# Full 128-row products at unit ends, issued as two 64-row halves with a lent PSUM bank

## The chip, the cores and the metric

The kernel runs on one core of a Trainium2 chip. The metric is device time in microseconds of one execution, the median of several runs. The engines are named as the profile names them: PE (TensorE; PEld are its weight loads), DVE (VectorE), ACT (ScalarE), POOL (GpSimd), SP (SyncE, which issues most DMAs). They run side by side, each in its own program order, and wait for each other through semaphores.

## The reference

Two attention layers over the same x (2048 tokens, width 512, 32 heads of 16) are mixed token by token with a gate. A is full softmax attention. B works in four segments of 512 tokens: causal softmax attention inside a segment, plus a read of a memory that the segments before it have built.

```python
def _A_ref(x, wqkv, wo):
    ...
    scores = jnp.einsum("bhqd,bhkd->bhqk", q, k) * scale
    p = _softmax(scores, axis=-1)
    o = jnp.einsum("bhqk,bhkd->bhqd", p, v)
    return (lambda x, *d: x.transpose(*d))(o, 0, 2, 1, 3).reshape(B, S, D) @ wo

def _B_ref(x, wq, wk, wv, wo, beta):
    ...
    for s in range(N):
        qs, ks, vs = q[:, :, s], k[:, :, s], v[:, :, s]
        logits = jnp.einsum("bhqd,bhkd->bhqk", qs, ks) * scale + mask
        p = _softmax(logits, axis=-1)
        a_dot = jnp.einsum("bhqk,bhkd->bhqd", p, vs)
        ...
        o = g * a_mem + (1.0 - g) * a_dot
    ...
    return o @ wo

x = A_x
g = _sigmoid((x * gate_w).sum(-1, keepdims=True))
return g * _A_ref(x, A_wqkv, A_wo) + (1 - g) * _B_ref(x, B_wq, B_wk, B_wv, B_wo, B_beta)
```

## The kernel before, in words

**Precision.** Every product that needs full fp32 is written as three products of halves: each operand is split into a rounded fp32r part and the rest, and (rest, part), (part, rest), (part, part) are summed in one PSUM bank.

**Stages.** Up to about 280 us the kernel projects x to queries, keys and values (lines 332 to 908) and stores them in DRAM. The long part after that is the attention.

**Units, slots, bursts.** A unit is four heads of one layer for one chunk of 512 queries. A unit of A has 64 slots and a unit of B has 10; they alternate (`units`, `slots`, lines 105 to 113), so a pair has 74 slots and there are 2368 in all. The loop at line 1328 walks the slots. In slot n:

- `score_part` (line 1030) issues on PE one score product `st` (128 keys by 512 queries, 50 rows of one half of the array: rows 0 to 63 or 64 to 127), and on ACT its exponential into `p` (L1068). The scores have three PSUM banks, in the pool `st_ps`.
- `max_part` (line 263) issues on PE one product `sm` for a unit that comes LEAD = 96 slots later, in the other half of the rows, and on DVE its maxima (L275 for A; for B two masked pieces, L290, the second of them behind the next maximum of A). These have four banks, `banks`; `oldest` (line 253) picks the one whose last read was issued longest ago, by `read_last`, and `was_read` (line 257) notes a read. The maxima of a unit are needed before its scores, since they go into the rows that the exponent subtracts.
- Every third slot (BURST = 3) closes a burst. Then PE either issues values (`some_values`, line 1080: the product of `p` with v for all four heads in four column blocks, summed in the one bank `ops`), or, if the list `shared` holds anything, three products from it.

So PE runs three score-and-maximum pairs, then values or three products, and again.

**Unit ends.** When the last value of a unit is issued, `ops` is copied to `oraw` (L1106) and stored. A unit of A then fills `shared` with twelve products of 128 rows by 512 columns, which take the place of values in four bursts; this is called a group below:

- for chunk 0, `later_tile` (line 958): one tile of the queries of chunks 2 and 3. At its end (`done`) ACT copies `ops` to `full` (L962), POOL splits it, and SP stores it 12 slots later;
- for the other chunks, `output` (line 1241): half of the output product of 128 tokens of the chunk before. After the first half `keep` copies `ops` to `part` (L1259), after the second `leave` copies it to `res` (L1263), POOL adds the part (L1265), and SP stores the result 6 slots later.

All matmuls of these kinds go through the helper at line 155. The last chunk's output products use `banks` and not `ops`, at the end, when no maxima are left (`fill`, `close`).

**Order.** The order on each engine is that of the code: this is a hand-written schedule (`manual_schedule`). Work beside the loop is put into slots with `at`. `octet` (line 1138) scales eight heads of a finished pair of units on POOL and sends them through DRAM; its reciprocal is L1169. `loads` (line 319) posts the keys and queries for maxima 20 slots ahead, on SP.

Of the kernel before, what the change touches and what calls it, by code (L numbers as in the profile page):

```python
# [10 lines left out]
F32 = mybir.dt.float32  # L11
# [8 lines left out]
D = 512  # L20
# [27 lines left out]
def gated_mix(ctx, tc, x, xT, wqkv, a_wo, b_wq, b_wk, b_wv, b_wo, beta, gate_w, out):  # L48
    nc = tc.nc
# [63 lines left out]
    nS = len(slots)  # L113
# [4 lines left out]
    for k in range(NU):  # L118
# [3 lines left out]
        start, apart = (33, (3, 3)) if k == 1 else (6, (9, 3)) if k < NU - 1 else (23, (3, 3))  # L122
# [3 lines left out]
        for m in range(len(maxs), len(maxs) + 64 + 10 * len(bs)):  # L126
            r = (m + 1) % 2
# [12 lines left out]
    def raw(t):  # L140

        return t[:].bitcast(F32)
# [10 lines left out]
    def matmul(*args, **kw):  # L153

        behind[0] = nc.tensor.matmul(*args, **kw)  # L155
# [95 lines left out]
    read_last = dict(zip(range(4), range(4)))  # L251

    def oldest():

        return min(read_last, key=read_last.get)

    def was_read(b):

        if b is not None:
            read_last[b] = count[0] = count[0] + 1  # L260
# [659 lines left out]
    fr = ctx.enter_context(tc.tile_pool(name="fr", bufs=1, reuse_waits="tile"))  # L920
# [4 lines left out]
    banks = [sm_ps.tile([128, CH], F32, name=f"sm{i}") for i in range(4)]  # L925

    ops = o_ps.tile([128, CH], F32, name="ops")

    halved = {}
# [25 lines left out]
    def x_later(c):  # L955
        return xT[:, c * CH:(c + 1) * CH]

    def later_tile(c, o):

        def done():  # L960
            full = fr.tile([128, CH], F32, tag="part", name="full")
            nc.scalar.copy(full, ops)  # L962
            t = fr.tile([128, 2, 2, 2, 128], F32R, tag="blk", name="qhalves", bufs=2)
            t = t.rearrange("p a o h t -> p a (o h t)")
            nc.gpsimd.tensor_copy(t[:, 0], full)
            nc.gpsimd.tensor_sub(t[:, 1], full, t[:, 0].bitcast(F32))
            for i in range(2):
                at(n + 12, lambda i=i: nc.sync.dma_start(
                    qd["A", o, c][16 * i:16 * i + 16].rearrange("d h t -> (d h) t"), raw(t[:, i])))


            if o == NO - 1 and c == LATER[0]:
                for i in range(2):
                    load_halves(("x", LATER[1]), "B", x_later(LATER[1]), (2 * i, 2 * i + 1), n + 2 + 18 * i,
                                [n + 24 + 29 * i, n + 28 + 29 * i])
            elif o == NO - 1:
                for i, (side, w) in enumerate((("A", a_wo), ("B", b_wo))):
                    load_halves(side, side, w, (0, 1), n + 2 + 18 * i, [n + 22 + 8 * i, n + 26 + 8 * i])
                    for k in range(2, 4):
                        load_halves(side, side, w, (k,), n + 50 + 22 * i + 3 * (k - 2), [n + 62 + 18 * i + 5 * (k - 2)])  # L980

        def f(i):
            k, (a, b) = i // 3, ((1, 0), (0, 1), (0, 0))[i % 3]
            assert {("q", k), (("x", c), k)} <= ready
            matmul(ops, halved["q"][:, k, a, o * 128:(o + 1) * 128], halved["x", c][:, k, b],
                             start=(i == 0), stop=(i == 11))
            if i == 11:
                done()
        for i in range(12):
            yield lambda i=i: f(i)  # L990
# [33 lines left out]
    def from_bank(n):  # L1024

        return nc.vector.tensor_copy if n > wide.start + 4 else nc.scalar.copy
# [108 lines left out]
    def at(n, f):  # L1135
        beside.setdefault(n, []).append(f)
# [78 lines left out]
    def products(ps, t, b, side, o, start, stop):  # L1215

        assert (side, o) in ready
        for i, (x, w) in enumerate(((1, 0), (0, 1), (0, 0))):
            yield lambda i=i, x=x, w=w: matmul(ps, t[:, b, x], halved[side][:, o, w], start=start and i == 0,
                                                         stop=stop and i == 2)  # L1220

    def out_rows(c, b):
        return out[c * CH + b * 128:c * CH + (b + 1) * 128, :]
# [31 lines left out]
    part = {}  # L1255

    def keep(ps, c, b):
        part[b] = fr.tile([128, D], F32, tag="part", name="part")
        nc.scalar.copy(part[b], ps)  # L1259

    def leave(ps, c, b):
        t = fr.tile([128, D], F32, tag="res", name="res", bufs=2)
        from_bank(n)(t, ps)  # L1263
        if b in part:
            nc.gpsimd.tensor_add(t, t, part.pop(b))  # L1265
        at(n + 6, lambda: nc.sync.dma_start(out_rows(c, b), t))

# [31 lines left out]
    def close(n, side, o, b):  # L1301
        for i in range(3):
            def f(i=i):
                assert (side, o, last) in scaled
                list(products(banks[b], closed[side, o], b, side, o, (side, o) == closing[0], (side, o) == closing[-1]))[i]()
            fill.append((n, f))
# [20 lines left out]
    n = 0  # L1327
    while n < nS or queue or beside or filled[0] < len(fill):
# [5 lines left out]
        if m < nS:  # L1334
            loads(m + PRE)

            b = oldest()
# [29 lines left out]
    for b in range(4):  # L1367
# [3 lines left out]
        t = fr.tile([128, D], F32, tag="v" if b % 2 else "res", name="res", bufs=2)  # L1371
# [37 lines left out]
```

## Time and profile before

| | |
|---|---|
| median of 3 runs | 1747.57 us (1745.27 to 1747.68) |
| span of the profiled execution | 1744.5 us; what lies around it, against the median: 3.1 us |
| granted TensorE clock | 1.000 |
| exponentials, L1068 | 2261, 600 ns each |
| maxima of A, L275 | 2048, 683 ns each |
| maxima of B, L290 | 512 pieces, 482 ns each in the mean |
| products of the groups (360) | 387 to 506 ns each as recorded |
| copies of `ops` at group ends (L962, L1259, L1263) | 8 of 589 ns, 11 of 589 ns, 11 of 604 ns |

The times of one instruction go from its start to its end; the next on the same engine can start before that end, so the distance of two starts is read from the order of time. The end of a matmul is modelled. A matmul that waits for another engine shows this on its weight load (PEld). Values are recorded as two passes each.

### The profile page before, as it was taken

To read this page: it belongs to the slowest core of one execution; us is meant where nothing else is said; L and a number is where in the kernel's file an instruction comes from. 1 tells how busy PE (TensorE), PEld (TensorE's weight loads), DVE (VectorE), ACT (ScalarE), POOL (GpSimd) and SP (SyncE) were. 2 spreads that over 40 slices of the span, in tenths; PEclk is the share of its full clock that TensorE was granted. 3 is DMA by queue.
4 is the path that set the end of the run, shared out by engine and by line. 5 is a ranking of instruction groups with operands and counts; after the bars stand their busy time and mean duration, and the time that the engine had idled before them with its cause. 6 is when DMAs were issued, how large, how long until landed. Compare 5 with 4: busy or idle time off the path is not lost.

```text
span 1744.5 us, 41555 instructions
## 1 busy us (share of the span) xinstructions
PE 1738.4 (100%) x15205; PEld 885.8 (51%) x15205; DVE 1597.1 (92%) x3327; ACT 1436.5 (82%) x2763; POOL 736.5 (42%) x992
## 2 busy tenths in 40 slices
PE   9999999999999999999999999999999999999999
PEld 7887775444444444444444444444444444444445
DVE  7757788999999999999999999999999999999931
ACT  6545557888888898888888888888888888888884
POOL 3543233234352427352534353535344353535443
PEclk9999999999999999999999999999999999999999
DMA  6787567335453446454545454444445444545542
GB/s 209 251 291 227 194 226 215 110 102 145 127 153 105 138 119 183 131 137 136 143 122 157 122 143 130 134 145 122 149 130 148 130 127 124 148 115 147 149 154 63
DMA packets 149387, 261.62 MB, mean 150 GB/s; under 512 B 39064, under 2 KB 61624, under 8 KB 148672
## 3 DMA queue, kind: packets, MB, share of 16 engines
q1 hardware_dynamic: 146640, 254.42, 49.2%
q0 software_dynamic: 2400, 4.29, 0.9%
q8 instruction: 121, 1.98, 0.5%
q14 instruction: 82, 0.67, 0.1%
q10 hardware_dynamic: 144, 0.26, 0.1%
HBM read 174.39 MB, written 83.25 MB: 148 GB/s over the span
## 4 chain that ended last, share of the span: by engine, by line
PE 99%; ACT 0%; DMA 0%; DVE 0%; issue 0%; SPq 0%; ACTq 0%; DVEq 0%
PE ops L155 40%; PE st L1045 28%; PE sm L242 14%; PE pr L366 9%; PE pair L366 4%; PE sm L155 2%; PE mt_ps L232 0%; PE tps L831 0%; PE sm L1045 0%; DMA vs<-wqkv 0%; PE mps L845 0%; PE num L804 0%; PE den L808 0%; ACT p L1068 0%; DVE pm L275 0%
## 5 line engine op out<-in xcount | busy, mean ns | idle before, releaser
L1068 ACT ACTIVATE p<-st 128x512 f32<-128x512 f32 x2261 | 1190.7, 600 | 147.6 <-PE sm L242 98.6
L275 DVE TENSOR_REDUCE pm<-sm 128x1 f32<-128x512 f32 x2048 | 1276.5, 683 | 9.7 <-PE sm L242 8.7
L242 PE MATMUL sm<-kA,qA 48*128 48x512 f32 x2048 | 662.5, 424 | 0.1
L1045 PE MATMUL st<-qA,kA 50*128 50x512 f32 x2014 | 656.2, 432 | 0.0
L155 PE MATMUL ops<-p,vA 128*17 128x256 f32 (+3 forms) x6360 | 553.0, 445 | 0.0
L1045 PEld LDWEIGHTS st<-qA,kA 50*128 50x128 f32 x2014 | 326.8, 185 | 423.4 <-ACT p L1068 378.9
L242 PEld LDWEIGHTS sm<-kA,qA 48*128 48x128 f32 x2048 | 337.8, 185 | 11.3 <-DVE ph L449 3.9
L1169 POOL TENSOR_TENSOR rcp<-rec,minus 128x32 f32<-128x32 f32 x43 | 234.8, 5461 | 78.3 <-DMA rec<-dend 73.5
L290 DVE CUSTOM_DVE_ANT_0 rest<-sm,mask 128x128 f32<-128x128 f32 (+3 forms) x512 | 246.8, 482 | 0.8 <-PE sm L242 0.7
L155 PEld LDWEIGHTS ops<-p,vA 128*17 128x17 f32 x6360 | 129.2, 96 | 216.1 <-issue 185.0
L1049 POOL TENSOR_SCALAR_AFFINE_SELECT p<-p 128x512 f32<-128x512 f32 x128 | 79.4, 637 | 270.4 <-ACT p L1068 265.7
L242 PE MATMUL sm<-kB,qB 48*128 48x128 f32 (+3 forms) x512 | 166.1, 384 | 0.0
L1045 PE MATMUL st<-qB,kB 50*128 50x512 f32 (+1 forms) x495 | 105.4, 330 | 0.3 <-ACT mt L235 0.3
L1045 PEld LDWEIGHTS st<-qB,kB 50*128 50x128 f32 x495 | 68.6, 186 | 62.2 <-ACT p L1068 50.5
L155 PE MATMUL ops<-p,vB 128*17 128x128 f32 (+3 forms) x1504 | 88.3, 350 | 0.0
L242 PEld LDWEIGHTS sm<-kB,qB 48*128 48x128 f32 x512 | 79.9, 184 | 0.0
L214 POOL TENSOR_TENSOR dm<-pm 128x32 f32<-128x32 f32 x32 | 7.9, 247 | 169.9 <-DVE pm L275 169.9
L437 POOL TENSOR_SCALAR mn<-full 128x512 f32<-128x512 f32 x24 | 36.7, 1527 | 75.6 <-ACT full L432 75.6
L223 POOL CAST ms<-pm 128x16 fp32r<-128x16 f32 x32 | 6.3, 196 | 127.5 <-DVE pm L290 127.5
L1185 POOL TENSOR_TENSOR v<-v,inv 128x512 f32<-128x512 f32 x31 | 39.8, 1283 | 28.1 <-DMA inv<-rdA 21.9
L155 PEld LDWEIGHTS ops<-p,vB 128*17 128x17 f32 x1504 | 33.8, 96 | 30.1 <-issue 26.1
L440 DVE TENSOR_TENSOR q<-full,q 128x512 fp32r<-128x512 f32 x40 | 29.2, 731 | 18.6 <-ACT q L433 15.8
(319 smaller groups left out, 1690.9 us busy)
## 6 DMA issues: line engine op xcount, KB each, us to landing
kA<-kdA SPq DMA_DIRECT2D x256, 128.0 KB
vA<-vdA SPq DMA_DIRECT2D x31, 544.0 KB
kA<-kdA SPq DMA_DIRECT2D x256, 64.0 KB
qB<-qdB SPq DMA_DIRECT2D x192, 64.0 KB
kB<-kdB SPq DMA_DIRECT2D x192, 64.0 KB
kdA<-q SPq DMA_DIRECT2D x32, 256.0 KB
qdB<-q SPq DMA_DIRECT2D x32, 256.0 KB
qA<-qdA SPq DMA_DIRECT2D x64, 128.0 KB
```

The lines of the kernel that those rows point to most:

```text
L155: behind[0] = nc.tensor.matmul(*args, **kw)
L242: nc.tensor.matmul(ps[:, n0:n0 + n], rows(qt[u][:, :, s * 128:(s + 1) * 128], h, 48), rows(k[:, :, k0:k0 + n], h, 48), start=True, stop=True)
L275: nc.vector.tensor_reduce(pm[:, h, s, kc:kc + 1], ps, axis=AX.X, op=ALU.max, negate=True)
L290: nc.vector.tensor_tensor_reduce(out=tri["rest"][:, 0:w], in0=ps[:, n0:n0 + w], in1=tri["mask"][:, CH - w:], scale=-1.0, scalar=3.0e38, op ...
L366: nc.tensor.matmul(ps, l, r, start=start, stop=stop)
L437: nc.gpsimd.tensor_scalar_min(ph["mn"], full, 0.0)
L440: nc.vector.tensor_sub(q2, full, q1.bitcast(F32))
L1045: nc.tensor.matmul(ps[:, n0:n0 + CH - q0], rows(k[:, :, b * 128:(b + 1) * 128], h, 50), rows(q[:, :, q0:], h, 50), start=True, stop=True)
L1049: nc.gpsimd.affine_select(out=x, in_=x, pattern=[[0, 4], [1, 128]], base=0, channel_multiplier=-1, compare_op=ALU.is_ge, fill=0.0)
L1068: nc.scalar.activation(p[:, h], ps, AF.Exp, scale=SCALE)
L1169: eng.tensor_tensor(r, rec, minus, op=ALU.pow)
L1185: eng.tensor_mul(k["v"], k["v"], k["inv"])
```

## The change

The twelve products of a group are issued as halves: rows 0 to 63 of both operands into `ops`, rows 64 to 127 into a second bank, and the two sums are added at the end. The second bank is one of the four of the maxima: `row_halves` takes the oldest at the first product and marks it as not to be had; `join_halves` copies both banks on ACT (the second to a new tile `bot`), gives the bank back, and adds the two on POOL. The stores of the result are put three slots later.

```diff
+    lent = [None]
+
+    def row_halves(l, r, start, stop):
+        if start:
+            lent[0] = oldest()
+            read_last[lent[0]] = 9 * nS
+        for i, ps in enumerate((ops, banks[lent[0]])):
+            rs = slice(64 * i, 64 * i + 64)
+            matmul(ps, l[rs], r[rs], start=start, stop=stop)
+
+    def join_halves(t):
+        bot = fr.tile([128, D], F32, tag="bot", name="bot")
+        nc.scalar.copy(t, ops)
+        nc.scalar.copy(bot, banks[lent[0]])
+        was_read(lent[0])
+        nc.gpsimd.tensor_add(t, t, bot)
...
             full = fr.tile([128, CH], F32, tag="part", name="full")
-            nc.scalar.copy(full, ops)
+            join_halves(full)
...
-                at(n + 12, lambda i=i: nc.sync.dma_start(
+                at(n + 15, lambda i=i: nc.sync.dma_start(
...
-            matmul(ops, halved["q"][:, k, a, o * 128:(o + 1) * 128], halved["x", c][:, k, b],
-                             start=(i == 0), stop=(i == 11))
+            row_halves(halved["q"][:, k, a, o * 128:(o + 1) * 128], halved["x", c][:, k, b], i == 0, i == 11)
...
-            yield lambda i=i, x=x, w=w: matmul(ps, t[:, b, x], halved[side][:, o, w], start=start and i == 0,
-                                                         stop=stop and i == 2)
+            l, r, first_, last_ = t[:, b, x], halved[side][:, o, w], start and i == 0, stop and i == 2
+            if ps is ops:
+                yield lambda a=(l, r, first_, last_): row_halves(*a)
+            else:
+                yield lambda l=l, r=r, first_=first_, last_=last_: matmul(ps, l, r, start=first_, stop=last_)
...
     def keep(ps, c, b):
         part[b] = fr.tile([128, D], F32, tag="part", name="part")
-        nc.scalar.copy(part[b], ps)
+        join_halves(part[b])

     def leave(ps, c, b):
         t = fr.tile([128, D], F32, tag="res", name="res", bufs=2)
-        from_bank(n)(t, ps)
+        if ps is ops:
+            join_halves(t)
+        else:
+            from_bank(n)(t, ps)
...
-        at(n + 6, lambda: nc.sync.dma_start(out_rows(c, b), t))
+        at(n + 9, lambda: nc.sync.dma_start(out_rows(c, b), t))
```

The order of PE at the end of the first output group, before: the fourth product burst and the burst behind it. `st` are scores, `sm0` to `sm3` the four banks of the maxima, `ops` the products with the weight `wB`.

```order
L1045 MATMUL st_9187<-qA11_8007,kA4_196 128x512
L242 MATMUL sm3_3294<-kA1_193,qA21_8648 128x512
L1045 MATMUL st_9195<-qA11_8007,kA4_196 128x512
L242 MATMUL sm1_3292<-kA1_193,qA21_8648 128x512
L155 MATMUL ops_3295<-wB_8668,blk_8885 128x512 x3
L1045 MATMUL st_9209<-qA11_8007,kA4_196 128x512
L242 MATMUL sm2_3293<-kA2_194,qA21_8648 128x512
L1045 MATMUL st_9214<-qA11_8007,kA4_196 128x512
L242 MATMUL sm3_3294<-kA2_194,qA21_8648 128x512
L1045 MATMUL st_9220<-qA11_8007,kA4_196 128x512
L242 MATMUL sm0_3291<-kA2_194,qA21_8648 128x512
```

The same two bursts of the change, first the product burst, then the burst behind it:

```order
L1063 MATMUL st_9316<-qA11_8112,kA4_196 128x512
L242 MATMUL sm0_3291<-kA1_193,qA21_8768 128x512
L1063 MATMUL st_9324<-qA11_8112,kA4_196 128x512
L242 MATMUL sm2_3293<-kA1_193,qA21_8768 128x512
L155 MATMUL ops_3295<-wB_8788,blk_9005 128x512
L155 MATMUL sm3_3294<-wB_8788,blk_9005 128x512
L155 MATMUL ops_3295<-wB_8788,blk_9005 128x512
L155 MATMUL sm3_3294<-wB_8788,blk_9005 128x512
L155 MATMUL ops_3295<-wB_8788,blk_9005 128x512
L155 MATMUL sm3_3294<-wB_8788,blk_9005 128x512
```

```order
L1063 MATMUL st_9344<-qA11_8112,kA4_196 128x512
L242 MATMUL sm0_3291<-kA2_194,qA21_8768 128x512
L1063 MATMUL st_9349<-qA11_8112,kA4_196 128x512
L242 MATMUL sm1_3292<-kA2_194,qA21_8768 128x512
L1063 MATMUL st_9355<-qA11_8112,kA4_196 128x512
L242 MATMUL sm2_3293<-kA2_194,qA21_8768 128x512
L155 MATMUL ops_3295<-p_9187,vB_8895 17x384 x4
L1063 MATMUL st_9364<-qA11_8112,kA4_196 128x512
L242 MATMUL sm3_3294<-kA2_194,qA21_8768 128x512
```

Three products have become six, in `ops` and `sm3` by turns. The maxima meanwhile go round three banks: the last maximum ahead of the products is in `sm2`, and `sm2` is used again by the third maximum of the next burst, three later; before, `sm1` held the last one ahead of the products and the three behind it use the other banks. `sm3` comes back one burst later.

The order of ACT at the same place, before:

```order
L1068 ACTIVATE p_9186<-st_9187 128x512
L1068 ACTIVATE p_9186<-st_9195 128x512
L1259 COPY part_9207<-ops_3295 128x512
L1068 ACTIVATE p_9186<-st_9209 128x512
L1068 ACTIVATE p_9186<-st_9214 128x512
```

and now:

```order
L1086 ACTIVATE p_9315<-st_9316 128x512
L1086 ACTIVATE p_9315<-st_9324 128x512
L972 COPY part_9339<-ops_3295 128x512
L973 COPY bot_9340<-sm3_3294 128x512
L1086 ACTIVATE p_9315<-st_9344 128x512
L1086 ACTIVATE p_9315<-st_9349 128x512
```

A second copy stands between the products' end and the exponentials of the next burst. On DVE no instruction is added or taken away; only the numbers of the banks that it reads are others.

## The prediction

> **What bounds the kernel now.** First the busy line of the page, then busy time by stretch, then what the instructions of the long stretch cost and wait for, then the order of time at one place.
>
> ```profile
> PE 1738.4 (100%) x15205; PEld 885.8 (51%) x15205; DVE 1597.1 (92%) x3327; ACT 1436.5 (82%) x2763; POOL 736.5 (42%) x992
> 350.00:1669.00 1319.00, 1318.95 (x12380) 599.87 (x12376) 1317.61 (x2821) 1175.91 (x2278) 574.91 (x785) 1.00 0.48 135
> L275 DVE TENSOR_REDUCE pm<-sm 128x1 f32<-128x512 f32 x1861 | 1159.6, 683 | 0.6
> DVE rest L290 <- PE sm L242: 0.7, 1, 0.7
> PEld st L1045 <- ACT p L1068: 406.4, 790, 0.9
> ```
>
> The second row is the stretch from 350 to 1669 us: length, then busy PE, PEld, DVE, ACT, POOL. All 30 product groups but the first lie in it. Two engines look full. PE's busy time is modelled and says little; DVE's 1317.61 of 1319.00 is measured, and its whole recorded idle time before maxima is 1.3 us (the third and fourth row). So **the maxima on DVE set the pace**, ACT at 89% does not, and an edit that leaves DVE's work alone can win only what DVE still loses. The last row says that PE is held by the exponentials often, so PE, ACT and DVE are close to each other. How close is read in order of time, first ACT and DVE, then PE, around the end of the group at 685 us (the last product at 691.48):
>
> ```profile
> 690.51 1.58 ACT L1068 ACTIVATE p<-st 128x512 f32<-128x512 f32 x3 [0.26 <-PE st L1045]
> 691.97 0.59 ACT L1259 COPY part<-ops 128x512 f32<-128x512 f32 x1
> 692.45 3.14 ACT L1068 ACTIVATE p<-st 128x512 f32<-128x512 f32 x6
> 695.90 1.57 ACT L1068 ACTIVATE p<-st 128x512 f32<-128x512 f32 x3 [0.30 <-PE sm L242]
> ...
> 690.12 0.69 DVE L275 TENSOR_REDUCE pm<-sm 128x1 f32<-128x512 f32 x1
> 692.01 4.27 DVE L275 TENSOR_REDUCE pm<-sm 128x1 f32<-128x512 f32 x7
> ...
> 705.90 8.21 DVE L275 TENSOR_REDUCE pm<-sm 128x1 f32<-128x512 f32 x13
> ...
> 690.61 0.39 PE L242 MATMUL sm<-kA,qA 48*128 48x512 f32 x1
> 690.92 0.96 PE L155 MATMUL ops<-wB,blk 128*128 128x512 f32 x3
> 691.81 0.50 PE L1045 MATMUL st<-qA,kA 50*128 50x512 f32 x1
> 691.81 0.50 PE L242 MATMUL sm<-kA,qA 48*128 48x512 f32 x1
> 692.15 0.40 PE L242 MATMUL sm<-kA,qA 48*128 48x512 f32 x1
> 692.39 0.40 PE L1045 MATMUL st<-qA,kA 50*128 50x512 f32 x1
> 692.39 0.40 PE L242 MATMUL sm<-kA,qA 48*128 48x512 f32 x1
> 692.72 0.84 PE L155 MATMUL ops<-p,vB 128*17 128x384 f32 x8
> 693.49 0.50 PE L1045 MATMUL st<-qA,kA 50*128 50x512 f32 x1
> 693.83 0.76 PE L1045 MATMUL st<-qA,kA 50*128 50x512 f32 x2
> 694.10 0.50 PE L242 MATMUL sm<-kA,qA 48*128 48x512 f32 x1
> 694.53 0.84 PE L155 MATMUL ops<-p,vB 128*17 128x128 f32 x16
> ```
>
> Columns: start, us, engine, line, operation, how many merged. Four things are read here.
>
> - Seven reductions in 4.27 us, one alone 0.68: (4.27 - 0.68) / 6 = **0.598 us per maximum**, with no gap. Thirteen at that rate would be 7.86; the row at 705.90 shows 8.21. So DVE loses 0.35 us there without any idle time recorded: its instructions overlap by 0.08 us, and a wait up to that length is hidden.
> - A score and a maximum stand side by side on PE (both at 692.39) and the next pair starts 0.24 later (692.15 to 692.39).
> - A copy on ACT takes 0.59, but the next starts after 692.45 - 691.97 = **0.48**; that is what one more copy in its queue costs.
> - From the last pair of a product burst to the next burst: 691.81 - 690.61 = 1.20 us, for the pair's own 0.24 and three products.
>
> **The change, part by part.** There are 30 groups of 12 products. The counts:
>
> ```profile
> L155 PE MATMUL ops<-wA,blk x132: 387/397/504, 685.4 to 1637.9; 128*128 128x512 f32 x132
> ...
> L155 PE MATMUL ops<-wB,blk x132: 387/397/498, 687.3 to 1639.7; 128*128 128x512 f32 x132
> L155 PE MATMUL ops<-wB,wA x96: 388/397/506, 322.6 to 645.1; 128*128 128x512 f32 x96
> ```
>
> (132 + 132 + 96) / 12 = 30. Of them 11 end in L1259, 11 in L1263, 8 in L962.
>
> *Products.* Three become six halves, alternately in the upper and the lower rows. Half products don't occur in this trace. The nearest row is the score-and-maximum pair: 0.24 for two matmuls of 512 columns in different row halves and different banks. At the other end, six in a row at 0.24 each are 1.44. I take 0.24 per pair, since those rows have the same rows, banks and columns: 0.24 + 3 x 0.24 = 0.96 instead of 1.20, **0.24 saved per burst** and 0.96 per group on PE.
>
> The Trainium skill, "TensorEngine Tiling (Array Packing)", section Tiling Modes, Key Properties, says that a change of tiling mode drains TensorE; the 1.20 against 0.96 agrees, and by that rule alone every saving would count (rival B).
>
> *The lent bank.* Maxima have four banks in turn, three while one is lent. A maximum then waits for the read of the one three before, not four. The third pair of each burst feels it: the maximum at 690.61 can start only when DVE has read the one that it starts at 690.12: 690.12 + 0.69 = 690.81, and a handover between the engines. That is +0.20 or a little more, against 0.24 saved: the next burst starts at about 691.8 again. So the bank **eats the saving**, burst for burst; in the burst after the group the lent bank comes back last, so its third maximum waits too: 692.01 + 0.68 = 692.69 for 692.39, +0.30. DVE itself isn't starved inside the group: results stay 0.2 to 0.3 us ahead of it, as now.
>
> *The second copy on ACT.* It stands behind the first, ahead of the exponentials, so the six at 692.45 start at 692.93. The third of them, now ending at 692.45 + 2 x 0.51 + 0.60 = 694.07 (0.51 is (3.14 - 0.60) / 5), frees the score bank of the matmuls at 694.10; +0.48 puts those at 694.57, and the values at 694.53 and all of PE behind them by 0.48. The 0.30 of the bank lies inside this. PE has nothing to catch up with: it is full with values and scores. So PE is late by **0.48**, and the question is what DVE has in hand.
>
> *What DVE has in hand.* Slots come three to a burst and 74 to a pair of units, so groups are of three kinds, ten of each. After the group at 685, DVE starves already (the row at 705.90): nothing in hand, 0.48 lost. After that at 775:
>
> ```profile
> 794.54 0.50 PE L242 MATMUL sm<-kB,qB 48*128 48x512 f32 x1
> 795.13 0.68 DVE L290 CUSTOM_DVE_ANT_0 rest<-sm,mask 128x512 f32<-128x512 f32 x1
> ```
>
> the result is there at 795.04 and wanted at 795.13: at most 0.09 in hand, less a handover, so 0.39 to 0.48 lost; I take 0.44. The group at 730:
>
> ```profile
> 729.54 3.67 DVE L275 TENSOR_REDUCE pm<-sm 128x1 f32<-128x512 f32 x6
> 733.22 0.29 DVE L290 CUSTOM_DVE_ANT_0 rest<-sm,mask 128x128 f32<-128x128 f32 x1
> ```
>
> Six maxima from 729.54 end their turn at 733.13, the next starts at 733.22: here DVE starves inside the group, 0.09 and about 0.07 more behind it. The faster products cure these 0.16, and let the group end some 0.2 earlier, so that of ACT's 0.48 only 0.2 reaches PE. Net about 0.15 lost.
>
> *POOL and SP.* The join adds one 128x512 addition per group, and the stores are posted three slots later. POOL is 44% busy (574.91 of 1319). Where it is tightest:
>
> ```profile
> 737.16 1.28 POOL L1265 TENSOR_TENSOR res<-res,part 128x512 f32<-128x512 f32 x1 [2.17 <-ACT res L1263]
> 738.38 5.47 POOL L1169 TENSOR_TENSOR rcp<-rec,minus 128x32 f32<-128x32 f32 x1
> ...
> 744.90 0.25 POOL L1175 TENSOR_TENSOR rec<-rec,gA 128x32 f32<-128x32 f32 x1
> 746.61 0.37 SPq L1178 DMA_DIRECT2D rdA<-rec  x1
> ```
>
> the reciprocals are 1.28 + 0.48 later, done at 746.9 where SP sends them at 746.61 now: 0.3 on SP's queue, ahead of loads that are posted 20 slots (12 us) early. I take nothing; uncovered, it is rival D.
>
> *Sum.* 10 x (0.48 + 0.44 + 0.15) = 10.7 us. The span of 1744.5 becomes 1755.2. The median of the runs is 1747.57, 3.1 above that span; it becomes **1758.3**. The part before 350 us and the tail after 1669 keep their work.
>
> The Trainium skill, same page, section Performance Considerations, PSUM Bottleneck, warns that tiling speeds up TensorE but not the emptying of PSUM, which may become the bottleneck. It speaks against this change, as the ACT rows do; by it, with whole copies of 0.59, the sum would be 30 x 0.59 = 17.7 and the time 1765.
>
> **The rivals.**
>
> *A. The delay is absorbed: no change, 1747.6.* ACT idles 0.30 before the exponentials at 695.90; if PE doesn't run behind it, the 0.48 shrinks before DVE has used the 0.3 to 0.4 us that it holds just after the group. For it: the third pair at 694.10 comes 0.27 after 693.83 and not 0.24, so ACT holds PE barely. Against: PE is full after it, and 705.90 and 794.54 show it at DVE's limit.
>
> *B. PE's saving outlasts the group: faster.* It decides if the lent bank doesn't hold the third pair, or if PE keeps a lead. 120 bursts x 0.24 = 29 us on PE; but DVE can give back only what it loses: 1.4 idle (1319.00 - 1317.61) and, per three groups, 0.35, 0.16 and perhaps 0.1 hidden, some 6. That is 7 at most: 1740 to 1743, say 1741. Against: with four banks no lead survives, since the row at 705.90 starves 14 us after a group.
>
> *C. The halves don't run side by side.* 0.24 + 1.44 for 1.20 is +0.48 per burst, with ACT's copy some 2 us per group: 60, **1808**. Against: the pairs at 692.39.
>
> *D. POOL reaches PE.* Each late reciprocal holds SP for up to 1.76 and a load behind it becomes due: 11 groups of L1263 x 1.76 = 19, on top 1778. Against: 12 us of lead on loads.
>
> **How the numbers follow.** The forecast has 0.50 (1752 to 1766), A 0.21, B 0.15, D 0.09, C 0.05. Measurements of this kernel can tell about 0.2% (3.5 us) from no change. Faster is B, 0.15; same is A, 0.21; slower the rest, 0.64. The range 1740 to 1770 leaves out C, most of D and a little of B. The forecast's own range is 1752 to 1766.
>
> **What would show it.** In the changed profile: 22 + 8 copies of about 0.59 from a maxima bank, each 0.48 behind the first; the next burst after a product burst 0.96 to 1.2 after its last pair; the third maximum of each lent burst waiting for DVE; and after groups of the first and third kind rows of reductions with more than 0.598 each, without much idle time recorded. DVE's share from 350 to the end of its maxima falls and that stretch grows by about 11 us, while the stretches before and after keep their length. Wrong it is if the stretch is not longer, if ACT's exponentials catch up within two bursts, or if six halves take over 1 us.

## The result and the profile after

| | before | after |
|---|---|---|
| median of 5 runs | 1745.97 us (1745.27 to 1747.68) | 1760.24 us (1760.17 to 1760.53) |
| span of the profiled execution | 1744.5 us | 1758.8 us |
| granted TensorE clock | 1.000 | 1.000 |

The change makes the kernel slower: the ratio after to before is 1.0079, with an interval of 1.0066 to 1.0091. The span grew by 14.3 us; the forecast was 10.7. The forecast time, 1758.3, is only 1.9 below the 1760.24, less than the 3.6 that the change itself was forecast too small. That is luck: the forecast was added to a median of three runs, 1747.57, and the median of five is 1.6 lower.

First the busy line of the page of the changed kernel, and one of its groups (line, engine, operation, output and input, count, then busy time and mean ns, then the idle time before them and what ended most of it):

```profile
PE 1752.2 (100%) x15565; PEld 925.9 (53%) x15565; DVE 1608.4 (91%) x3327; ACT 1449.0 (82%) x2793; POOL 774.9 (44%) x1022
L275 DVE TENSOR_REDUCE pm<-sm 128x1 f32<-128x512 f32 x2048 | 1283.0, 682 | 10.4 <-PE sm L242 8.7
```

Then the changed kernel's busy time by stretch, with the same columns as in the prediction:

```profile
350.00:1683.00 1333.00, 1333.00 (x12730) 639.14 (x12726) 1329.33 (x2821) 1188.34 (x2306) 611.84 (x814) 1.00 0.47 133
1683.00:1759.00 76.00, 71.64 (x474) 37.97 (x472) 8.16 (x16) 49.77 (x101) 30.18 (x36) 1.00 0.35 110
```

The stretch of the maxima went from 1319 to 1333 us, and the tail of 76 us is the same: nearly all of the loss lies in the stretch of the groups. DVE has the same 2821 instructions there, but their busy time went from 1317.61 to 1329.33. Of the 14 us, 11.7 stand in the records as work of DVE, and only 2.3 as idle time (of the 10.4 us of idle time in the second row above, 9.0 lie ahead of 350 us, as they do before). That is the hidden wait of which the prediction spoke: the next reduction starts late by some 0.08 us, again and again, and hardly a gap shows.

The lent bank shows at PE, in the waits of its weight loads (engine, tile and line, waited for: us in total, times, longest). Before:

```profile
PEld sm L242 <- DVE pm L275: 1.3, 4, 0.4
```

After:

```profile
PEld sm L242 <- DVE pm L275: 28.8, 94, 0.4
```

So 94 maxima wait 0.31 us each in the mean for DVE to read a bank; 4 did before.

Now the end of the group at 685, in order of time, DVE first. The changed kernel:

```profile
693.52 0.68 DVE L275 TENSOR_REDUCE pm<-sm 128x1 f32<-128x512 f32 x1
...
695.41 4.38 DVE L275 TENSOR_REDUCE pm<-sm 128x1 f32<-128x512 f32 x7
...
709.99 12.56 DVE L275 TENSOR_REDUCE pm<-sm 128x1 f32<-128x512 f32 x20
```

The first row is the reduction that starts at 690.12 before, so the change is 3.40 us late as this group ends. The seven that took 4.27 take 4.38. The last row is the one at 705.90 before: 4.09 late. **One group has cost 0.69 us**, and nearly all of it in the 16 us behind it. The row also tells who sets the pace there: (12.56 - 0.68) / 19 = 0.625 us per maximum. Before, the row at 705.90, followed for four reductions more than in the prediction:

```profile
705.90 10.75 DVE L275 TENSOR_REDUCE pm<-sm 128x1 f32<-128x512 f32 x17
```

(10.75 - 0.68) / 16 = 0.629. DVE alone needs 0.598. In this row it is thus fed at PE's pace, in both kernels. Ahead of it finished maxima lie waiting, so that a delay of PE reaches DVE step by step: the reductions are still 3.40 us late at 693.81 of the kernel before, 3.72 at 696.20, 3.90 at 699.81 and 4.08 at 703.40.

This is not so everywhere. Behind the groups at 730 and 775, before:

```profile
750.26 13.84 DVE L275 TENSOR_REDUCE pm<-sm 128x1 f32<-128x512 f32 x23
...
795.74 13.84 DVE L275 TENSOR_REDUCE pm<-sm 128x1 f32<-128x512 f32 x23
```

(13.84 - 0.68) / 22 = 0.598, DVE's own pace. Of the 1379 distances between two neighbouring reductions of A from 350 to 1669 us, 47 are above 0.62, and 45 of these lie in short stretches behind the groups like 685 (707 to 714 us for this one). So DVE goes at its own pace nearly all the time. Still it has next to nothing in hand: the shortest time for which a finished maximum waits for DVE behind a group is 0.07 us in groups like 685, 0.07 to 0.10 in those like 730 and 0.08 to 0.11 in those like 775 (0.06 in the last), where 0.07 is what is seen when DVE is the one that waits (the ends of matmuls are modelled). Once in each stretch between two groups, then, a delay of PE reaches DVE almost whole.

ACT at the same place in the changed kernel:

```profile
695.54 0.59 ACT L972 COPY part<-ops 128x512 f32<-128x512 f32 x1
696.02 0.59 ACT L973 COPY bot<-sm 128x512 f32<-128x512 f32 x1
696.50 3.07 ACT L1086 ACTIVATE p<-st 128x512 f32<-128x512 f32 x6
```

Less the 3.40, the first copy starts at 692.14 where it was 691.97: **0.17 late**. The second starts 0.48 behind it, and the exponentials 0.65 late (696.50 - 3.40 = 693.10 for 692.45). And PE:

```profile
694.00 0.40 PE L1063 MATMUL st<-qA,kA 50*128 50x512 f32 x1
694.26 0.49 PE L242 MATMUL sm<-kA,qA 48*128 48x512 f32 x1
694.27 0.49 PE L155 MATMUL sm<-wB,blk 64*128 64x512 f32 x1
694.60 0.39 PE L155 MATMUL ops<-wB,blk 64*128 64x512 f32 x1
694.60 0.40 PE L155 MATMUL sm<-wB,blk 64*128 64x512 f32 x1
694.83 0.39 PE L155 MATMUL ops<-wB,blk 64*128 64x512 f32 x1
694.84 0.39 PE L155 MATMUL sm<-wB,blk 64*128 64x512 f32 x1
695.06 0.39 PE L155 MATMUL ops<-wB,blk 64*128 64x512 f32 x1
695.07 0.49 PE L242 MATMUL sm<-kA,qA 48*128 48x512 f32 x1
695.29 0.51 PE L1063 MATMUL st<-qA,kA 50*128 50x512 f32 x2
...
696.14 0.49 PE L242 MATMUL sm<-kA,qA 48*128 48x512 f32 x1
...
698.58 0.84 PE L155 MATMUL ops<-p,vB 128*17 128x128 f32 x16
```

The third maximum of the product burst stands at 694.26, 0.26 behind its score: it waited for its bank. It works in the upper 64 rows. The lower half of the first product (into `sm`) starts beside it, at 694.27, although the program has it behind the upper half; the upper half, in the same rows as the maximum, starts only at 694.60. From then on both go in steps of 0.23. So the last upper half starts 0.80 after the maximum, where the last whole product started 691.48 - 690.61 = 0.87 after it. The maximum is 0.25 late (694.26 - 3.40 = 690.86 for 690.61), the saving up to the last product is 0.07, and the rest, 0.18, is what the first copy is late. Behind the copies all follows: the values at 698.58 are 0.65 late (695.18 for 694.53).

The groups at 730 and 775 by the same reading. DVE as the groups run, before:

```profile
728.93 4.28 DVE L275 TENSOR_REDUCE pm<-sm 128x1 f32<-128x512 f32 x7
...
778.98 0.69 DVE L275 TENSOR_REDUCE pm<-sm 128x1 f32<-128x512 f32 x1
```

and ACT at their ends, before:

```profile
736.47 0.60 ACT L1263 COPY res<-ops 128x512 f32<-128x512 f32 x1
736.96 3.23 ACT L1068 ACTIVATE p<-st 128x512 f32<-128x512 f32 x6
...
781.92 0.59 ACT L1259 COPY part<-ops 128x512 f32<-128x512 f32 x1
782.40 3.14 ACT L1068 ACTIVATE p<-st 128x512 f32<-128x512 f32 x6
```

The same reductions after:

```profile
733.02 4.28 DVE L275 TENSOR_REDUCE pm<-sm 128x1 f32<-128x512 f32 x7
...
783.49 0.68 DVE L275 TENSOR_REDUCE pm<-sm 128x1 f32<-128x512 f32 x1
```

and ACT after:

```profile
740.52 0.59 ACT L972 COPY res<-ops 128x512 f32<-128x512 f32 x1
741.00 0.59 ACT L973 COPY bot<-sm 128x512 f32<-128x512 f32 x1
741.48 3.06 ACT L1086 ACTIVATE p<-st 128x512 f32<-128x512 f32 x6
...
786.36 0.59 ACT L972 COPY part<-ops 128x512 f32<-128x512 f32 x1
786.84 0.59 ACT L973 COPY bot<-sm 128x512 f32<-128x512 f32 x1
787.32 3.16 ACT L1086 ACTIVATE p<-st 128x512 f32<-128x512 f32 x6
```

At 730 the change is 4.09 late on the way in (733.02 - 728.93); the copy comes 0.04 early (740.52 - 4.09 = 736.43 for 736.47), the exponentials 0.43 late. At 775 it is 4.51 late (783.49 - 778.98); the copy comes 0.07 early, the exponentials 0.41 late.

To see whether these three speak for the other 27, the starts of the 2,560 reductions, which are the same and in the same order in both kernels, were subtracted one by one, and the step of this difference from group to group taken. The prediction's three kinds of groups are called by the group shown of each. The median of the ten groups of a kind, for the change and for the experiments below (all on the profiled executions):

| kernel | over before, us | ratio and interval | 685-kind | 730-kind | 775-kind |
|---|---|---|---|---|---|
| forecast | 10.7 | | 0.48 | 0.15 | 0.44 |
| the change | 14.3 | 1.0079 (1.0066 to 1.0091) | 0.66 | 0.42 | 0.42 |
| e1, no second copy | 7.1 | 1.0040 (1.0025 to 1.0055) | 0.34 | 0.11 | 0.31 |
| e2, before + a copy | 15.4 | 1.0090 (1.0075 to 1.0105) | 0.53 | 0.49 | 0.51 |
| e2b, before + two copies | 35.0 | 1.0198 (1.0183 to 1.0213) | 1.17 | 1.16 | 1.11 |
| e3, before, bank withheld | 18.0 | 1.0104 (1.0089 to 1.0119) | 0.69 | 0.48 | 0.66 |
| e4, no POOL addition | 14.4 | 1.0083 (1.0066 to 1.0100) | 0.65 | 0.43 | 0.42 |
| e5, upper rows only | -2.2 | 0.9989 (0.9980 to 0.9999) | -0.02 | -0.20 | -0.09 |
| e7, second copy later | 11.5 | 1.0064 (1.0049 to 1.0079) | 0.48 | 0.23 | 0.38 |
| e8, before + a copy later | 9.3 | 1.0058 (1.0043 to 1.0073) | 0.31 | 0.31 | 0.26 |
| e9, lower bank first | 18.2 | 1.0103 (1.0088 to 1.0118) | 0.71 | 0.49 | 0.62 |
| e10, free half's bank first | 15.7 | 1.0088 (1.0071 to 1.0105) | 0.70 | 0.49 | 0.38 |
| e11, free half issued first | 10.6 | 1.0058 (1.0041 to 1.0075) | 0.44 | 0.23 | 0.42 |

The second column is the difference of the medians (of the change, of 1760.24 and 1745.97). In the change every group but one costs, and the sizes of a kind lie within 0.13 us of each other. The one outlier: the group at 639 has a step of -0.40, because a single idle time of 0.74 us, at 673 in before, is not there in the change. Why it went was not tried; it also fails to appear in e1, e4, e7 and e9 to e11.

### The profile page after: what moved, and what is told of

Same layout as the page of the kernel before. It is cut to its first block, busy times and chain, and to the rows that moved or that the text cites. A ratio compares the mean times of both kernels' runs of the same rounds, so it can differ in the third digit from the quotient of the medians.

```text
span 1758.8 us, 42363 instructions
## 1 busy us (share of the span) xinstructions
PE 1752.2 (100%) x15565; PEld 925.9 (53%) x15565; DVE 1608.4 (91%) x3327; ACT 1449.0 (82%) x2793; POOL 774.9 (44%) x1022
## 4 chain that ended last, share of the span: by engine, by line
PE 99%; ACT 0%; DMA 0%; DVE 0%; issue 0%; ACTq 0%
PE ops L155 36%; PE st L1063 28%; PE sm L242 16%; PE pr L366 9%; PE pair L366 4%; PE sm L155 4%; PE mt_ps L232 0%; PE tps L831 0%; PE sm L1063 0%; DMA vs<-wqkv 0%; PE mps L845 0%; PE num L804 0%; PE den L808 0%; ACT p L1086 0%; DVE pm L275 0%
## 5 line engine op out<-in xcount | busy, mean ns | idle before, releaser
L275 DVE TENSOR_REDUCE pm<-sm 128x1 f32<-128x512 f32 x2048 | 1283.0, 682 | 10.4 <-PE sm L242 8.7
L242 PE MATMUL sm<-kA,qA 48*128 48x512 f32 x2048 | 709.2, 433 | 0.1
L1063 PEld LDWEIGHTS st<-qA,kA 50*128 50x128 f32 x2014 | 330.7, 185 | 401.1 <-ACT p L1086 362.1
L1063 PEld LDWEIGHTS st<-qB,kB 50*128 50x128 f32 x495 | 75.7, 186 | 47.9 <-ACT p L1086 32.3
```

The costliest lines, as they stand in the source:

```text
L242: nc.tensor.matmul(ps[:, n0:n0 + n], rows(qt[u][:, :, s * 128:(s + 1) * 128], h, 48), rows(k[:, :, k0:k0 + n], h, 48), start=True, stop=True)
L275: nc.vector.tensor_reduce(pm[:, h, s, kc:kc + 1], ps, axis=AX.X, op=ALU.max, negate=True)
L1063: nc.tensor.matmul(ps[:, n0:n0 + CH - q0], rows(k[:, :, b * 128:(b + 1) * 128], h, 50), rows(q[:, :, q0:], h, 50), start=True, stop=True)
```

## The experiments

### The parts of the change, one by one

**e1: no second copy.** Bank and halves stay, the copy to `bot` and the addition go.

```diff
     def join_halves(t):
-        bot = fr.tile([128, D], F32, tag="bot", name="bot")
         nc.scalar.copy(t, ops)
-        nc.scalar.copy(bot, banks[lent[0]])
         was_read(lent[0])
-        nc.gpsimd.tensor_add(t, t, bot)
```

> The change without the second copy on ACT and without the addition on POOL; the lent bank is given back at the same place. The rows 64 to 127 of the products are left out of the result. Theory 1 (the second copy puts ACT and then PE back by 0.48 us per group and DVE has nothing in hand): most of the 14.3 us is gone; what stays is the wait of the third maximum for its bank in the burst behind the group, some 0.1 to 0.2 us per group: 1747 to 1752 us. Theory 2 (the lent bank or the halves themselves cost the time): 1757 to 1761 us. Theory 3 (the addition on POOL delays work behind it): this run alone cannot tell it from theory 1.

Measured: 1753.11 us (1752.99 to 1753.20) beside 1746.06, 7.1 over. This is between the two expectations: half of the loss goes with the copy, half stays. What stays at 685 is 0.34, about the 0.30 that the prediction worked out for the third maximum of the burst behind the group. So bank and halves are no even trade on PE even without a copy.

**e2: the kernel before with one more copy.** Whole products, four banks; at each group's end ACT copies a constant tile to `bot`.

```diff
+    def copies(t):
+        nc.scalar.copy(t, ops)
+        for i in range(1):
+            nc.scalar.copy(fr.tile([128, D], F32, tag="bot", name="bot"), tri["mask"])
...
-        nc.scalar.copy(part[b], ps)
+        copies(part[b])
```

> The kernel before with one more 128x512 copy on ACT behind each of the 30 copies at group ends; whole products, no bank lent, the copy's result is not used. Theory 1: PE late by 0.4 to 0.5 us per group and nothing in hand on DVE, +11 to +14 us: 1757 to 1760 us. Theory 2 and theory 3: 1745 to 1749 us.

Measured: 1761.49 us (1761.40 to 1762.55), 15.4 over, or 0.51 per group, with little difference between the kinds. The exponentials behind the extra copy start 0.50 to 0.52 late, and to 0.02 all of it reaches DVE: rival A has fallen, and DVE has nothing to speak of in hand in any kind of group.

**e3: the kernel before with a bank withheld.** Whole products; from a group's first product to its copy one bank of the maxima lies idle.

```diff
+    def lend(start):
+        if start:
+            lent[0] = oldest()
+            read_last[lent[0]] = 9 * nS
+    def copied(t):
+        nc.scalar.copy(t, ops)
+        was_read(lent[0])
...
+                if ps is ops:
+                    lend(k == ks[0] and n == 0)
```

> The kernel before with whole products into one bank, but one bank of the maxima kept unused from a group's first product to its copy. Theory 1 says that the halves' saving of 0.24 us per burst and the bank's wait of 0.20 to 0.25 cancel: with the wait and without the saving each group should lose some 0.3 to 0.6 us, 1755 to 1764 us. If the bank costs nothing by itself: 1745 to 1749 us.

Measured: 1764.10 us (1764.04 to 1764.88), 18.0 over, 0.69, 0.48 and 0.66 per group. The loan alone is dearer than the whole change. With the halves and without a copy (e1) it costs 7.1: the halves do win back most of the bank's price, 10.9 of 18.0, but no more.

The prices of e1 and e2, 7.1 and 15.4, add up to 22.5, and the change costs 14.3. They lie beside each other: in the burst behind a group PE waits for the third maximum's bank (e1) and for the exponentials behind the second copy, and the later of the two counts. In the change at 685 that third maximum is 0.35 late (696.14 - 3.40 = 692.74 for 692.39), the exponentials are 0.65 late, and DVE's step is 0.66 to 0.69.

**e4: no addition on POOL.** `bot` is copied, but not added.

```diff
-        nc.gpsimd.tensor_add(t, t, bot)
```

> The change with both copies on ACT but without the addition on POOL; the rows 64 to 127 of the products are left out of the result. Theory 1 and theory 2: as the change, 1759 to 1761 us. Theory 3: 1756 us or less.

Measured: 1760.43 us (1760.32 to 1760.63), the same as the change (1760.24). The 30 additions cost nothing, and with them the core of rival D has fallen. The stores stay three slots later here; no run moves them back alone, but at 685 the 0.65 of the exponentials makes up the group's whole step, so that nothing is left for them.

**e5: half of the products, and nothing else.** The kernel before with only the upper rows of each product: no bank lent, no copy, no join. It is the saving on PE without any price.

```diff
-            matmul(ops, halved["q"][:, k, a, o * 128:(o + 1) * 128], halved["x", c][:, k, b],
+            matmul(ops, halved["q"][0:64, k, a, o * 128:(o + 1) * 128], halved["x", c][0:64, k, b],
...
+            rs = slice(0, 64 if ps is ops else 128)
```

> The kernel before with the products of the groups cut to rows 0 to 63, into one bank, with no bank lent and no second copy: the saving on PE without any of its price. The rows 64 to 127 of these products are left out of the result. Theory 1 (the maxima on DVE set the pace, so time that PE gains at a group's end cannot be kept): 1742 to 1746 us, no more than DVE loses now (some 7 us), in all likelihood the 0.16 us per three groups and the single stall at 674 us. Theory 4 (PE sets the pace, so every saved 0.2 us per burst counts, 120 bursts): 1722 us or less.

Measured over 10 runs: 1743.45 us (1742.49 to 1747.28) beside 1745.67, 2.2 under; the ratio is 0.9989 (0.9980 to 0.9999). Of the 0.96 per group that PE was to save, 0 to 0.20 reach DVE. By the row behind the group at 685 the saving is gone (order of time, DVE, of e5):

```profile
705.37 10.75 DVE L275 TENSOR_REDUCE pm<-sm 128x1 f32<-128x512 f32 x17
```

It is the row of before to the hundredth, 17 reductions in 10.75 us. Inside the group PE does gain: measured against DVE, the group's copy starts 0.42 us early. But the third maximum of the burst behind it is only 0.25 early, and those from 697 on 0.03 to 0.04. One place where the lead ends is seen in PE's waits for banks, with all four banks in use (the same line as above, 1.3 us before):

```profile
PEld sm L242 <- DVE pm L275: 20.4, 54, 0.4
```

PE runs ahead into banks that DVE has not read yet, for DVE goes at its own 0.598 there. Rival B has fallen, and with it any form of the halving that saves no more on PE than this: freed of all its costs it is worth 0.1%.

### Is the price of a copy its place?

**e2b: two more copies.** As e2, with two copies of the constant tile.

```diff
-        for i in range(1):
+        for i in range(2):
```

> The kernel before with two more 128x512 copies on ACT behind each of the 30 copies at group ends, their result not used. Theory 1 (each copy puts the chain back by its 0.48 us, nothing is absorbed): twice the 15.4 us that one copy cost, 1774 to 1778 us. If ACT catches up in its idle time, the second copy costs clearly less than the first or more than it by what was absorbed: 1764 to 1772 us or above 1780 us.

Measured: 1780.69 us (1779.38 to 1780.98), 35.0 over. The second extra copy costs 35.0 - 15.4 = 19.6 us, 0.65 per group, more than the first. By the expectation this would mean that a part of the first had been absorbed. ACT at the end of the group at 685 says otherwise (e2b):

```profile
701.60 0.59 ACT L960 COPY part<-ops 128x512 f32<-128x512 f32 x1
702.08 1.27 ACT L962 COPY bot<-mask 128x512 f32<-128x512 f32 x2
703.26 2.05 ACT L1074 ACTIVATE p<-st 128x512 f32<-128x512 f32 x4
```

One such copy takes 0.62, so the second starts 1.27 - 0.62 = 0.65 behind the first: it waits for its end (a wait for ACT's own semaphore stands there in the trace), since both write `bot`, of which the pool `fr` holds one buffer (`bufs=1`). The exponentials start 703.26 - 701.60 = 1.66 behind the group's copy instead of 0.48, which is 1.18 late, and the steps at DVE are 1.11 to 1.17. So the copies cost what they take in ACT's queue, nothing of note is absorbed, and the 0.65 is of this experiment's making.

**e8: the extra copy four slots later.** As e2, but the constant's copy stands behind the first exponentials of the next burst.

```diff
+        at(n + 4, lambda: nc.scalar.copy(fr.tile([128, D], F32, tag="bot", name="bot"), tri["mask"]))
```

> The kernel before with one more 128x512 copy on ACT for each of the 30 groups, four slots after the copy at the group's end: behind the next burst's exponentials. Theory 1: ACT's idle time of 0.30 us ahead of the burst after that takes up part of it, 0.1 to 0.25 us per group stay: 1749 to 1754 us. If the place doesn't matter: 1760 to 1762 us, as with the copy at the group's end.

Measured: 1754.95 us (1754.05 to 1759.82), 9.3 over, a little above what was expected. The same copy costs 0.3 instead of 0.5 there, ahead of the 0.30 that ACT idles at 695.90 in before.

**e7: the change with the second copy four slots later.** The copy to `bot`, the bank's return, the addition and the stores move.

```diff
-        nc.scalar.copy(bot, banks[lent[0]])
-        was_read(lent[0])
-        nc.gpsimd.tensor_add(t, t, bot)
...
+        def join():
+            bot = fr.tile([128, D], F32, tag="bot", name="bot")
+            nc.scalar.copy(bot, banks[lent[0]])
+            was_read(lent[0])
+            nc.gpsimd.tensor_add(t, t, bot)
+            then()
+        at(n + 4, join)
...
```

> The change with the second copy (and all that follows from it: giving the bank back, the addition, the split, the stores) four slots later, behind the exponentials of the next burst and not ahead of them; the lent bank is away for one burst longer. Theory 1 in the form that only the copy's place counts: about as without a second copy, 1752 to 1755 us. Theory 1 with the bank's wait as a second price of nearly the same size, which the longer loan repeats: 1756 to 1763 us.

Measured: 1757.16 us (1756.87 to 1757.22), 11.5 over, inside the second expectation. Beside its own runs of the kernel before it wins 2.8 us from the change and stays slower than before, as e1 says it must.

### Which half ends the group?

The change's PE rows say that the half in the rows of the waiting maximum ends last. In groups like 775 that maximum stands in the lower rows, and the upper half runs beside it (the changed kernel, PE):

```profile
785.30 0.50 PE L242 MATMUL sm<-kA,qA 48*128 48x512 f32 x1
785.30 0.72 PE L155 MATMUL ops<-wB,blk 64*128 64x512 f32 x2
785.64 0.39 PE L155 MATMUL sm<-wB,blk 64*128 64x512 f32 x1
785.87 0.39 PE L155 MATMUL ops<-wB,blk 64*128 64x512 f32 x1
785.87 0.62 PE L155 MATMUL sm<-wB,blk 64*128 64x512 f32 x2
```

Here `ops` is done first, at 785.87 + 0.39 = 786.26, and its copy starts at 786.36. That would explain why the copy is early at 775 and late at 685. Three kernels try it.

**e9 and e10: the copies in another order.** e9 copies the lent bank first in every group, e10 only where the last maximum is in the upper rows. The edit of e10 (`upper` holds whether the last maximum issued stands in the upper rows):

```diff
+        upper[0] = r == 0
...
-        nc.scalar.copy(t, ops)
-        nc.scalar.copy(bot, banks[lent[0]])
+        for half in ((1, 0) if upper[0] else (0, 1)):
+            nc.scalar.copy(bot if half else t, banks[lent[0]] if half else ops)
```

> The change, but ACT copies the lent bank (rows 64 to 127) first and ops second; nothing else. In the change's trace the half that has the rows of the waiting third maximum ends some 0.22 us behind the other half: the upper half in the groups at 685 and 730, the lower in those at 775. Theory 1 (the group's end for ACT is the end of the half that is copied first; every group then delays DVE by the lateness of that end plus 0.48): the delays per group go from 0.65 to 0.43 at 685, from 0.42 to 0.20 at 730, and from 0.42 to 0.64 at 775; the sum falls by 10 x 0.22 = 2.2 us, to some 1758 us where before is 1746 (12.3 us over before). Theory 2 (both halves end together as far as ACT is concerned, and only the two copies and the bank count): no difference from the change, 14.3 us over before, and the same delays per group.

> The change, but each group copies first the bank of the half in which no maximum stands: the lent bank where the last maximum is in the upper rows, ops where it is in the lower. Theory 1: 0.43 at 685, 0.20 at 730 and 0.42 at 775, 10.1 to 10.5 us over before (some 1756). Theory 2: as the change, 14.3 us over before. If it comes below 9 us over before, more than the first copy's start was held by the late half; if the gain is under 1.5 us, the wait of the third maximum in the burst behind the group (0.34, 0.11, 0.31 per group without any second copy) has become what ends last.

Measured: e9 1763.85 us (1763.65 to 1764.05) and e10 1761.35 (1760.92 to 1761.47) beside 1745.62. Both expectations missed: instead of 2 or 4 us less than the change, or nothing, they cost more. Only e9's groups like 775 do what its first theory said (0.62 for 0.64). The end of the group at 685 in e10 on PE:

```profile
695.01 0.39 PE L155 MATMUL sm<-wB,blk 64*128 64x512 f32 x1
695.24 0.39 PE L155 MATMUL ops<-wB,blk 64*128 64x512 f32 x1
...
696.96 0.84 PE L155 MATMUL ops<-p,vB 128*17 128x384 f32 x8
```

and on ACT:

```profile
695.75 0.58 ACT L976 COPY bot<-sm 128x512 f32<-128x512 f32 x1 [0.15 <-issue]
696.23 0.59 ACT L976 COPY part<-ops 128x512 f32<-128x512 f32 x1
```

The last lower half is recorded as done at 695.01 + 0.39 = 695.40, and yet the copy of its bank starts at 695.75, just behind the end of the upper half (695.63), which stands ahead of it in the program. So ACT learns of the second half's end only after the first's. The trace's record of the semaphore that PE raises agrees: between 694.95 and 695.64 it is not raised, and then twice, at 695.64 and 695.68. And `ops`, now copied second, is free only at 696.23 + 0.59 = 696.82, so that the values wait until 696.96: 0.23 later against DVE than in the change. Of this 0.04 is left in DVE's step (0.70 for 0.66).

**e11: the free half issued first.** If that reading is right, the free half must stand first in the program, sum in `ops`, and be copied first.

```diff
+    first_half = [False]
...
         if start:
             lent[0] = oldest()
             read_last[lent[0]] = 9 * nS
-        for i, ps in enumerate((ops, banks[lent[0]])):
+            first_half[0] = n + 9 + LEAD < nS and maxs[n + 9 + LEAD][1][0] == 0
+        for i, ps in zip((1, 0) if first_half[0] else (0, 1), (ops, banks[lent[0]])):
```

> The change, but in the groups whose last maximum stands in the upper rows (those like 685 and 730) the lower half of each product is issued ahead of the upper, sums in ops and is copied first; the groups like 775 stay as they are. The run before it showed that a half issued second is not seen as finished by ACT until the half issued first has ended, so that copying it first gained nothing and held ops longer. Theory 1 (ACT's first copy waits for the half that is issued first; issued first and free of the waiting maximum, it ends 0.22 us earlier): copy at 0.05 us before, not 0.17 behind, its old place at 685, delay per group 0.43 instead of 0.65; at 730 0.20 to 0.25 instead of 0.42; at 775 0.42 as in the change; 10 to 11 us over before, some 1756. Theory 2 (the delay is that of the third maxima and the copies, whichever half is first): as the change, 14.3 us over before.

Measured: 1756.31 us (1756.10 to 1756.63) beside 1745.71, 10.6 over, with 0.44, 0.23 and 0.42 per group: the first theory's numbers. The group at 685 in e11, first the reduction on DVE that starts at 690.12 before:

```profile
692.58 0.69 DVE L275 TENSOR_REDUCE pm<-sm 128x1 f32<-128x512 f32 x1
```

then ACT:

```profile
694.39 0.59 ACT L974 COPY part<-ops 128x512 f32<-128x512 f32 x1
694.88 0.59 ACT L975 COPY bot<-sm 128x512 f32<-128x512 f32 x1
695.35 3.17 ACT L1088 ACTIVATE p<-st 128x512 f32<-128x512 f32 x6
```

Late by 2.46 on the way in (692.58 - 690.12), the copy is 0.04 early (694.39 - 2.46 = 691.93 for 691.97) where it was 0.17 late, and the exponentials are 0.44 late. This takes 3.7 us off the change (14.3 against 10.6 over before), by the order of two instructions alone, and is the best of the forms of the halving that compute all of it; it is still slower than before.

## Why the prediction was right, and where its size was off

- **Direction and mechanism: right.** The kernel is slower, which had 0.64. ACT's second copy delays the exponentials, they delay PE, and DVE has nothing to meet it with. e2 shows the price of the copy (0.51 per group; 0.48 forecast), e4 that POOL's additions cost nothing, e5 that PE's saving is worth 0.1% even free of charge.
- **The products: nearly right.** Six halves take 695.29 - 694.26 = 1.03 us from the last pair to the next burst, for 0.96 forecast and 1.20 before. Rival C (1.44) has fallen. The prediction called it a sign of being wrong if six halves take over 1 us. From the first half's start to the next burst they take 695.29 - 694.27 = 1.02, but only because the first lower half slips ahead; the five behind it take 0.69. The halves start 0.34 behind a maximum in their own rows and 0.23 behind each other; the forecast had 0.24 throughout.
- **The lent bank: right in place and size** in the group at 685: the third maximum is 0.25 late in the product burst, and e1 has 0.34 where 0.30 was forecast for the burst behind it. That this "lies inside" the copy's 0.48 is right too: the change costs less than e1 and e2 together.
- **The mis-sized term: the end of the group.** The prediction let the saving of 0.24 cancel the bank's wait up to the end of the products, and, in groups like 730, "let the group end some 0.2 earlier, so that of ACT's 0.48 only 0.2 reaches PE". What ACT waits for is the last half that stands first in the program, the upper one. Where the late maximum is in the upper rows too, the saving up to that point is 0.07 and not 0.24. The group's copy starts 0.17 late at 685 and 0.04 early at 730 (there 0.12 late against DVE, which is 0.16 ahead by then, its starving cured). With the 0.48 this gives 0.65 and 0.44 of delay behind the group, and the steps measured are 0.66 and 0.42, for 0.48 and 0.15 forecast. DVE's starving inside the groups like 730 was cured as forecast (0.15 in the mean of the ten), but behind the group DVE is as late as PE is, and that swallows the cure. 10 x (0.66 - 0.48) + 10 x (0.42 - 0.15) = 4.5 us too few, less 0.2 for 775 and 0.8 for the idle time that vanished at 673: 3.5, of the 3.6 missing. e11 takes away just this lateness and lands at 10.6, close to the forecast's 10.7.
- **775: right by luck.** 0.44 was to come from 0.04 that DVE has in hand; e2 shows 0.51 of a delay of 0.52 arriving, so 0.01 was. The 0.42 are 0.48 less the 0.07 that the group ends early.
- **What bounds the kernel: right.** The maxima on DVE set the pace: 0.598 inside the groups and behind those like 730 and 775. Only for some microseconds behind the groups like 685 is DVE fed at PE's pace, 0.63 apart in the row at 705.90, and there the prediction read that it has nothing in hand. Both halves of the result follow. PE's saving is worthless, since DVE cannot go faster than its own pace; the copy's price is whole, since what DVE has in hand runs out once between any two groups. What was missed is only that the lost 0.35 us at 705.90 stays lost when PE is freed (e5 has the same row); what holds PE to 0.63 there was not tried.

The Trainium skill's "TensorEngine Tiling (Array Packing)", section Performance Considerations, PSUM Bottleneck, warned in the right direction. The 0.59 per copy that was put with it is too much: copies in ACT's queue start 0.48 apart, and e2 measures 0.51.

## What to carry to other kernels

A saving on one engine is worth what the next engine can take: here DVE went at its own pace for nearly the whole stretch, and PE's lead ended on banks that DVE had not read. An extra instruction on an engine that hands over work (here 0.5 us a piece, 30 times) counts at its full distance if the consumer's stock runs out even once before the next such place. When a product is split over two row halves, its end is that of the half that shares rows with whatever waits; issue the other half first and copy its bank first. Copying it first alone did not help (e10). A bank lent from a rotating set is not free because it is idle on average: here it cost 0.5 to 0.7 us a loan by itself.

## What was not expected of the hardware

- Matmuls in different row halves pass each other: at 694.27 a lower half starts 0.33 us before the upper half that the program has ahead of it. The Trainium skill, "TensorE: Matmul & The Clock Gate", section Part 3: Packing small matmuls — row/col tiling, says that matmuls keep the program's order in start and end. The starts here don't; the measurement decides.
- The end of a half that passed another is seen by ACT only after the other's: 695.75 for a half recorded as done at 695.40 (e10). In what other engines see, the order of ends that the same section states holds in this trace, and e11 gains by it. The ends of matmuls are modelled, so that the 0.35 is no more exact than they are.
- DVE's records show 99.7% busy (1329.33 of 1333) in a stretch that lost 14 us to waits.
- Copies on ACT start 0.48 apart when they write different tiles, and 0.65 apart when the second writes the one buffer that the first has just written (e2b, pool `fr`).
